# Loading K, wq and wo one stretch ahead, and a new order for the last head pair, in a one-core attention kernel

## The chip, the cores and the metric

The kernel runs on one core of a Trainium2 chip. The metric is the device time of one launch, in microseconds (us). "Span" is the stretch of the profile from the first to the last instruction, about 2 us shorter than the device time.

Engines are named as the profile names them: PE is TensorE (matmul), PEld its weight loads, DVE is VectorE, ACT is ScalarE, POOL is GpSimd, SP is SyncE. SPq, the queue of SP, issues nearly all DMAs of this kernel; they go out in program order, one after the other.

## The reference, cut to what matters

```python
xn = layernorm(x)                                # x: 2048 x 640, bf16
q  = xn @ wq                                     # 32 heads of 192
k, v = last 512 rows of k_cache, v_cache         # per head, 512 x 192
p  = softmax(q @ k.T * 192 ** -0.5)
s  = concat_heads(p @ v) @ wo                    # 6144 -> 640
g  = silu((silu(xn @ w_gate) * (xn @ w_up)) @ w_down)   # F = 1536
out = x + s * g
```

## The kernel before: the parts that matter

First comes the feed-forward part (until 168 us; it leaves `g2` in SBUF), then 16 pairs of heads. In a pair, PE computes scores for 4 contexts of 512 query rows (q for the next context is made between them), then PV for the 4 contexts, with output tiles (`wo_tile`) of two contexts earlier in between. K is centred over its rows, which needs K transposed (DMA transposes into `KT`), a sum of each of 3 chunks on DVE (`sum_k`) and an addition (`centre_k`).

```python
    for pr in range(NPAIR):                      # 16 pairs
        for b in range(NB):                      # 4 contexts
            i = pr * NB + b
            if b == 0:
                if pr < last:
                    load_k(pr + 1)
                load_v(pr)
                if pr < last:
                    load_wq(pr + 1)
                load_wo(pr)
                if pr >= last - 1:
                    for t in range(8):
                        load_xr(t + 8 if pr < last else t)
                        # ... (cut)
            for kc in range(KC):
                if kc < 3 and i + 1 < NS:
                    q_rows(i + 1, kc)            # PE, then a reduce on DVE into qT
                scores(i, kc)                    # PE, then an exp on ACT
                if pr < last:
                    if b == 1:
                        transpose_k(pr + 1, kc)  # a DMA transpose on SPq
                    elif b == 2 and kc < 3:
                        sum_k(pr + 1, kc)        # DVE
                    elif b == 3:
                        centre_k(pr + 1, kc)     # DVE
                        # ... (cut)
        # ... PV and output tiles of this pair (cut)
    i = last * NB
    for b in range(NB):                          # the last pair
        for q2 in range(2):
            if b >= 2:
                while stores:
                    store()                      # SPq
                wo_last(b - 2, 2 * q2)
                wo_last(b - 2, 2 * q2 + 1)
            pv(i + b, q2)                        # PE; O_b on ACT; transpose of O_b on SPq
```

An output tile of the last pair, `wo_last`, multiplies on DVE (`s_f`), adds on POOL or DVE, and writes into one of three `ob` buffers, which come free when their store has landed.

The softmax here doesn't subtract the row's maximum and nothing guards it: scores larger than these inputs give would overflow.

## Time and profile before

| | before |
|---|---|
| device time, median of 4 (range) | 963.70 us (963.48 to 966.59) |
| span | 962.5 us |
| PE busy / idle | 933.6 / 28.9 us |
| PE waits for the qT reduce | 12.6 us, 11 times |
| the one long wait in the tail | 5.5 us |

PE is the bottleneck. Part 1 of the page of the kernel before (busy time, share, instructions):

```profile
PE 933.6 (97%) x7970; PEld 588.0 (61%) x7970; DVE 572.0 (59%) x964; ACT 494.6 (51%) x867; POOL 63.6 (7%) x56
```

The Trainium skill (Perfetto Trace Analysis, section Identifying the Most-Contended Engine) warns that the busy share of matmuls says little about the distance to the limit. That holds here, so I measured how far apart matmuls *start* in undisturbed stretches: 108 ns on average for q and scores (they run in concurrent pairs of 64 rows, one pair every 216 ns), 83 ns for PV, 136 ns for output tiles. Whatever exceeds this is loss, including matmuls that count as busy but run at half clock.

The waits of PE in the kernel before (waiting engine and line, released by, total us, times, longest):

```profile
PE mm L415 <- DVE qT L420: 12.6, 11, 5.0
PE sc L491 <- DVE s_f L530: 5.5, 1, 5.5
PE mm L450 <- ACT O_b L460: 1.8, 3, 0.7
PE sc L429 <- ACT p_t L433: 0.7, 2, 0.5
```

The first line names the reduce, which takes 1.22 us and is not at fault. The timeline of the kernel before shows why it is late. In pair 14, which starts at 840.06 us, first the SP queue (start, duration in us):

```profile
842.04 1.46 SPq L93 DMA_DIRECT2D K_p<-in_A_k_cache_dram  x2
843.55 2.71 SPq L110 DMA_DIRECT2D V_p<-in_A_v_cache_dram  x2
846.30 3.28 SPq L104 DMA_DIRECT2D wq_p<-in_A_wq_dram  x5
849.63 0.52 SPq L117 DMA_DIRECT2D wo_p<-in_A_wo_dram  x1
850.20 4.19 SPq L482 DMA_DIRECT2D x_r<-in_A_x_dram  x8
854.57 5.10 SPq L130 DMA_TRANSPOSE KT<-K_p  x4
```

then DVE and PE in the same timeline (in brackets the idle time before, and what ended it):

```profile
860.85 0.69 DVE L137 TENSOR_REDUCE ssum<-KT 128x1 f32<-128x512 bf16 x1 [6.62 <-DMA KT<-K_p]
861.45 1.22 DVE L420 TENSOR_REDUCE qT<-mm 128x512 bf16<-128x1024 f32 x1
862.72 0.61 PE L415 MATMUL mm<-xnT,wq_p 64*128 64x512 bf16 x2 [5.01 <-DVE qT L420]
```

Read it backwards: PE waits 5.01 us for a reduce, the reduce stands behind a K sum on DVE, the K sum waits 6.62 us for a K transpose, and the transposes stand in the SP queue behind everything that the pair loads. In the ordinary pairs the x_r line is missing and PE waits at most 0.9 us (2.0 in pair 10).

The long wait of the tail, in the timeline of the kernel before:

```profile
919.67 13.64 SPq L464 DMA_TRANSPOSE OT_b<-O_b  x10
931.15 1.50 PE L450 MATMUL mm<-V_p,p_t 128*128 128x193 bf16 x16
933.40 1.00 SPq L537 DMA_DIRECT2D out_dram<-ob  x2
935.50 0.83 DVE L532 TENSOR_TENSOR ob<-s_f,sacc 128x640 bf16<-128x640 f32 x1 [5.76 <-DMA out_dram<-ob]
938.16 3.36 PE L491 MATMUL sc<-wo_p,OT_b 128*128 128x320 bf16 x12 [5.52 <-DVE s_f L530]
```

The DVE add waits for an `ob` buffer, so for a store, and the first store is issued at 933.40 only, behind ten transposes of O_b in the SP queue. Meanwhile the DVE can serve nothing else, and PE runs out of score buffers.

Both waits have a sequel. After them matmuls run at half clock: the 12 matmuls at 938.16 take 3.36 us, 1.79 elsewhere. The windows view of the kernel before (busy us of PE, PEld, DVE, ACT, POOL, then the granted clock, DMA share, GB/s):

```profile
857.00:868.00 11.00, 5.99 (x34) 2.44 (x31) 5.78 (x8) 2.96 (x3) 0.00 (x0) 0.72 0.16 31
931.00:942.00 11.00, 5.48 (x36) 3.85 (x34) 3.62 (x8) 2.92 (x8) 1.61 (x2) 0.77 0.38 106
```

The Trainium skill (TensorE: Matmul & The Clock Gate, Part 1) describes a gate that halves the array's clock after idleness and releases it after some 3.4 us of work. On the halving this trace agrees: after the wait in pair 14, pairs of matmuls start 427 ns apart, and 216 ns apart later. The release came after 5.9 us of work there, and after 3.3 us in pair 10.

### The profile page before, as it was taken

The page shows a single profiled execution, that of the slowest core. Times are in us where ns is not written, and L with a number is a line of the kernel's source. Part 1 is how long each engine was busy: PE and PEld are TensorE (multiplying, and loading weights), DVE is VectorE, ACT ScalarE, POOL GpSimd, SP SyncE. Part 2 cuts the span into 40 slices and gives each one's busy share as a digit, 9 for nine tenths or more (in the row PEclk, how much of TensorE's full clock was granted, in tenths as well). Part 3 has the DMA queues.
Part 4 walks back from the last instruction along what each step waited for, and adds up shares of the span by engine and source line. Part 5 has one row for each costly group of instructions (what it writes and reads, how often), then busy time and mean ns, then how long its engine had stood idle before and what let it go on. Part 6 is the DMA issues. An engine that isn't in the chain of part 4 may idle for free.

```text
span 962.5 us, 18723 instructions
## 1 busy us (share of the span) xinstructions
PE 933.6 (97%) x7970; PEld 588.0 (61%) x7970; DVE 572.0 (59%) x964; ACT 494.6 (51%) x867; POOL 63.6 (7%) x56
## 2 busy tenths in 40 slices
PE   9999999999999999999999999999999999979978
PEld 5455556575757575757575757574747474737555
DVE  6433320757666766666667666666676767656625
ACT  3222223666465646465646564645464646445651
POOL 0000000000000000000000000000000000006944
PEclk9999999999999999999999999999999999999998
DMA  9230500044434354535343434343343536362423
GB/s 299 57 72 20 119 17 1 1 73 85 85 74 80 78 85 73 86 72 91 68 88 70 92 66 86 71 86 72 62 97 58 100 56 102 54 158 33 126 56 104
DMA packets 240227, 76.32 MB, mean 79 GB/s; under 512 B 221200, under 2 KB 240144, under 8 KB 240144
## 3 DMA queue, kind: packets, MB, share of 16 engines
q1 hardware_dynamic: 239200, 74.32, 38.9%
q8 instruction: 62, 1.02, 0.4%
q10 hardware_dynamic: 944, 0.82, 0.3%
q14 instruction: 21, 0.17, 0.1%
HBM read 39.45 MB, written 2.62 MB: 44 GB/s over the span
## 4 chain that ended last, share of the span: by engine, by line
PE 81%; SPq 7%; DMA 5%; DVE 4%; issue 1%; ACT 1%; POOL 0%; DVEq 0%; ACTq 0%; POOLq 0%
PE sc L491 21%; PE mm L450 17%; PE mm L415 15%; PE sc L429 11%; PE sc L270 11%; PE mm L292 5%; SPq L130 4%; DMA KT<-K_p 4%; DVE qT L420 3%; SPq L104 2%; ACT O_b L460 1%; SPq L464 0%; DMA x_r<-in_A_x_dram 0%; ACT p_t L433 0%; DMA out_dram<-ob 0%
## 5 line engine op out<-in xcount | busy, mean ns | idle before, releaser
L433 ACT ACTIVATE p_t<-sc 128x1024 bf16<-128x1024 f32 x256 | 254.9, 1022 | 155.0 <-PE sc L429 154.4
L420 DVE TENSOR_REDUCE qT<-mm 128x512 bf16<-128x1024 f32 x189 | 230.9, 1222 | 95.9 <-PE mm L415 95.2
L460 ACT ACTIVATE O_b<-mm,r 128x192 bf16<-128x192 f32 x512 | 186.7, 417 | 180.4 <-DVE r L458 115.8
L415 PE MATMUL mm<-xnT,wq_p 64*128 64x512 bf16 x1890 | 239.0, 380 | 13.3 <-DVE qT L420 12.6
L491 PE MATMUL sc<-wo_p,OT_b 128*128 128x320 bf16 x1488 | 224.5, 300 | 5.9 <-DVE s_f L530 5.5
L429 PE MATMUL sc<-qT,khat 64*128 64x512 bf16 x1536 | 201.7, 378 | 1.2 <-ACT p_t L433 0.7
L450 PE MATMUL mm<-V_p,p_t 128*128 128x193 bf16 x2048 | 192.8, 247 | 2.0 <-ACT O_b L460 1.8
L450 PEld LDWEIGHTS <-p_t 128*128 128x128 bf16 x2048 | 174.2, 97 | 17.8 <-issue 9.2
L491 PEld LDWEIGHTS <-OT_b 128*128 128x128 bf16 x1488 | 144.2, 98 | 54.5 <-issue 5.7
L415 PEld LDWEIGHTS <-wq_p 64*128 64x128 bf16 x1890 | 95.3, 95 | 125.0 <-issue 24.3
L506 DVE TENSOR_TENSOR sacc<-sacc,sc 128x640 f32<-128x640 f32 x216 | 165.5, 808 | 0.0
L429 PEld LDWEIGHTS <-khat 64*128 64x128 bf16 x1536 | 79.4, 95 | 94.2 <-issue 8.0
L458 DVE RECIPROCAL r<-mm 128x2 f32<-128x2 f32 x256 | 43.7, 171 | 151.8 <-ACT O_b L460 106.0
L278 DVE TENSOR_TENSOR hT<-sc,sg 128x512 bf16<-128x512 f32 x47 | 32.5, 692 | 86.5 <-ACT sg L277 86.5
L509 POOL TENSOR_TENSOR sacc<-sacc,g_73 128x640 f32<-128x640 f32 x16 | 22.1, 1404 | 782.9 <-ACT O_b L460 782.9
L277 ACT ACTIVATE sg<-sc 128x512 bf16<-128x512 f32 x47 | 28.1, 597 | 77.6 <-PE sc L270 77.6
L270 PE MATMUL sc<-xnT,wu_sb 128*128 128x512 bf16 (+1 forms) x245 | 58.7, 370 | 0.0
L270 PE MATMUL sc<-xnT,wg_sb 128*128 128x512 bf16 (+1 forms) x245 | 58.7, 370 | 0.0
L292 PE MATMUL mm<-wd_sb,hT 128*128 128x320 bf16 x384 | 56.6, 299 | 0.0
L137 DVE TENSOR_REDUCE ssum<-KT 128x1 f32<-128x512 bf16 x48 | 32.6, 679 | 34.7 <-DMA KT<-K_p 34.7
L292 PEld LDWEIGHTS <-hT 128*128 128x128 bf16 x384 | 37.6, 98 | 18.9
L270 PEld LDWEIGHTS <-wu_sb 128*128 128x128 bf16 x255 | 24.9, 98 | 26.9
(51 smaller groups left out, 215.2 us busy)
## 6 DMA issues: line engine op xcount, KB each, us to landing
wo_p<-in_A_wo_dram SPq DMA_DIRECT2D x16, 480.0 KB, 4.6
K_p<-in_A_k_cache_dram SPq DMA_DIRECT2D x32, 192.0 KB, 3.4
V_p<-in_A_v_cache_dram SPq DMA_DIRECT2D x32, 192.0 KB, 3.7
wq_p<-in_A_wq_dram SPq DMA_DIRECT2D x64, 80.0 KB, 3.5
wq_p<-in_A_wq_dram SPq DMA_DIRECT2D x16, 160.0 KB, 3.7
x_r<-in_A_x_dram SPq DMA_DIRECT2D x16, 160.0 KB, 4.0
out_dram<-ob SPq DMA_DIRECT2D x16, 160.0 KB, 1.8
x_t<-in_A_x_dram SPq DMA_DIRECT2D x14, 160.0 KB, 3.0
```

What stands on the lines that cost most here:

```text
L130: nc.sync.dma_start_transpose(out=d["KT"][:, 0:3, j * P : (j + 1) * P], in_=d["K"][:, j, :, :].rearrange("p h d -> p (h d)"),)
L270: nc.tensor.matmul(out, w_sb[:, c, f * P : (f + 1) * P], xnT[:, c, qc], start=(c == 0), stop=(c == NC - 1),)
L292: nc.tensor.matmul(dn[:, 0:HD], hTs[b][:, f, ti * P : (ti + 1) * P], wd_sb[:, f, cols], start=(f == 0), stop=(f == NF - 1),)
L415: nc.tensor.matmul(q_ps[:, h, :], pairs[pr]["wq"][r, c, j * P : (j + 1) * P], xnT[r, c, b * 512 : (b + 1) * 512], start=(c == 0), stop=(c ...
L420: nc.vector.reduce_sum(qTs[i][:, j, :], q_ps[:, :, :].rearrange("p h n -> p n h"), axis=AX.X)
L429: nc.tensor.matmul(sc[:, h, :], khat[r, j, ks], qT[r, j, :], start=(j == 0), stop=(j == 2))
L433: nc.scalar.activation(p_t[:, :, :], sc[:, :, :], ACT.Exp, scale=scale)
L450: nc.tensor.matmul(acc[:, k, h * 256 : h * 256 + Dh + 1], Ps[i][kc][:, h, qt * P : (qt + 1) * P], V_p[:, kc, h, 0 : Dh + 1], start=(kc == ...
L458: nc.vector.reciprocal(r[:, k, :, :], a_k[:, :, Dh : Dh + 1])
L460: nc.scalar.activation(O_b[:, qt, h, :], a_k[:, h, 0:Dh], ACT.Copy, scale=r[:, k, h, :])
L491: nc.tensor.matmul(sc[:, n, 0:HD], OTs[i][:, 3 * qt + j, :], pairs[i // NB]["wo"][:, j, n * HD : (n + 1) * HD], start=(first and j == 0), ...
L506: nc.vector.tensor_tensor(s_t, s_t, sc[:, :, 0:HD], ALU.add)
```

## The change

The intent: K, wq and wo of the next pair are loaded during the PV stage before (or the feed-forward part), so that at the start of a pair the SP queue holds the K transposes first. In the last pair three contexts of PV come ahead of the first output tile; the first eight output tiles are written into the x_r tiles, which are done with by then, and not into shared buffers; O_b of these contexts is transposed two row tiles at a time, so by 6 DMA transposes and not 12; POOL takes more adds; the last context's first scores use PSUM buffers that q no longer needs; DVE normalises half of O_b; the last tile is handled in halves.

```diff
-                elif b == 3 and f < 5:
-                    centre_k(0, f)
+                elif b == 3:                     # feed-forward part
+                    if f < 5:
+                        centre_k(0, f)
+                    elif f < 8:
+                        (load_k, load_wq, load_wo)[f - 5]((1, 1, 0)[f - 5])
 ...
-        sc = sc_tile()
+        sc = mm_tile() if i == NS - 1 and kc < 2 else sc_tile()
 ...
+            if k == 0 and (i < 2 or (pr == last and b < NB - 1)):
+                nc.vector.tensor_tensor(O_b[...], a_k[...], r[...].to_broadcast([P, 2, Dh]), ALU.mult)
+                continue
 ...
-            if pr == last and b < NB - 1:        # a transpose for each row tile (3 blocks)
+        if pr == last and b < NB - 1:            # one for each two row tiles (6 blocks)
 ...
-            if b == 0:
-                if pr < last:
-                    load_k(pr + 1)
-                load_v(pr)
-                if pr < last:
-                    load_wq(pr + 1)
-                load_wo(pr)
-                # ... x_r loads
 ...
-                    if b == 1:
+                    if b == 0:
                         transpose_k(pr + 1, kc)
 ...
+            if b == 0:                           # after the context's scores
+                load_v(pr)
+                # ... x_r loads
 ...                                              # in the PV stage, after context b
+            if b == 0 and pr + 2 < NPAIR:
+                load_k(pr + 2)
+            elif b == 1 and pr + 2 < NPAIR:
+                load_wq(pr + 2)
+            elif b == 2:
+                load_wo(pr + 1)
 ...
-        ob = finp.tile([P, D], bf, name="ob", bufs=3)
+        ob = xrs[t] if b < 2 else finp.tile([P, D], bf, name="ob", bufs=4)
 ...
+    for b in range(NB - 1):
+        for q2 in range(2):
+            pv(i + b, q2)
+    for q2 in range(2):
+        wo_last(0, 2 * q2, G)
+        wo_last(0, 2 * q2 + 1, G)
+        pv(i + 3, q2)
+    for qt in range(4):
+        wo_last(1, qt, G)
+        store(3)
+        wo_last(2, qt, V if qt % 2 else G)
+        transpose_o(i + 3, qt)
+    for qt in range(4):
+        store(2)
+        wo_last(3, qt, G if qt < 2 else V)
+    store(0)
```

More of the change, by code (lines that the diff above doesn't have):

```diff
@@ L458, in pv @@
             nc.vector.reciprocal(r[:, k, :, :], a_k[:, :, Dh : Dh + 1])
+            if k == 0 and (i < 2 or (pr == last and b < NB - 1)):
+                nc.vector.tensor_tensor(
+                    O_b[:, qt, :, :], a_k[:, :, 0:Dh], r[:, k, :, :].to_broadcast([P, 2, Dh]),
+                    ALU.mult,
+                )
+                continue
             for h in range(2):
@@ L462, in pv @@
                 )
-            if pr == last and b < NB - 1:
-                nc.sync.dma_start_transpose(
-                    out=OT_b[:, 3 * qt : 3 * qt + 3, :],
-                    in_=O_b[:, qt, :, :].rearrange("p h d -> p (h d)"),
-                )
-        if pr < last and q2 == 1:
+        if pr == last and b < NB - 1:
+            nc.sync.dma_start_transpose(
+                out=OT_b[:, 6 * q2 : 6 * q2 + 6, :],
+                in_=O_b[:, 2 * q2 : 2 * q2 + 2, :, :].rearrange("p t h d -> p (t h d)"),
+            )
+        elif pr < last and q2 == 1:
             nc.sync.dma_start_transpose(
@@ L486, in late, with wo_mm @@
         return i // NB >= NPAIR - 2 and i % NB >= 2
-    def wo_mm(sc, i, qt, first=True, end=True):
-        for n in range(2):
-            for j in range(3):
-                nc.tensor.matmul(
-                    sc[:, n, 0:HD], OTs[i][:, 3 * qt + j, :],
-                    pairs[i // NB]["wo"][:, j, n * HD : (n + 1) * HD],
-                    start=(first and j == 0), stop=(end and j == 2),
-                )
+    def wo_mm(ps, i, qt, n, first=True, end=True):
+        for j in range(3):
+            nc.tensor.matmul(
+                ps, OTs[i][:, 3 * qt + j, :], pairs[i // NB]["wo"][:, j, n * HD : (n + 1) * HD],
+                start=(first and j == 0), stop=(end and j == 2),
+            )
     def wo_tile(i, qt):
@@ L500, in wo_tile @@
         sc = sc_tile()
-        wo_mm(sc, i, qt)
+        for n in range(2):
+            wo_mm(sc[:, n, 0:HD], i, qt, n)
         s_t = sacc[:, t, :].rearrange("p (n d) -> p n d", n=2)
@@ L516, with wo_last, store @@
     stores = []
-    def wo_last(b, qt):
+    def wo_last(b, qt, eng):
         i, t = last * NB + b, 4 * b + qt
-        end = b == NB - 1 and qt == 3
-        ob = finp.tile([P, D], bf, name="ob", bufs=3)
-        s_f = finp.tile([P, 2, HD], f32, name="s_f")
-        ob2 = ob[:].rearrange("p (n d) -> p n d", n=2)
-        s_t = sacc[:, t, :].rearrange("p (n d) -> p n d", n=2)
-        g_t = g2[:, t, :].rearrange("p (n d) -> p n d", n=2)
-        sc = sc_tile()
-        if late(i):
-            wo_mm(sc, i - NB, qt, end=False)
-        wo_mm(sc, i, qt, first=not late(i))
-        nc.vector.tensor_tensor(s_f[:], sc[:, :, 0:HD], g_t, ALU.mult)
-        pool = qt < 3 if b < 2 else qt % 2 == 0
-        (nc.gpsimd if pool else nc.vector).tensor_tensor(ob2, s_f[:], s_t, ALU.add)
+        ob = xrs[t] if b < 2 else finp.tile([P, D], bf, name="ob", bufs=4)
+        s_f = finp.tile([P, 2, HD], f32, name="s_f", bufs=3)
+        halves = [slice(n * HD, (n + 1) * HD) for n in range(2)]
+        split = b == NB - 1 and qt == 3
+        sc = None if split else sc_tile()
+        ps = [(mm_tile()[:, 0, :] if split else sc[:, n, :])[:, 0:HD] for n in range(2)]
+        for n, cols in enumerate(halves):
+            if late(i):
+                wo_mm(ps[n], i - NB, qt, n, end=False)
+            wo_mm(ps[n], i, qt, n, first=not late(i))
+            if split:
+                nc.vector.tensor_tensor(s_f[:, n, :], ps[n], g2[:, t, cols], ALU.mult)
+        if split:
+            for n, cols in enumerate(halves):
+                nc.vector.tensor_tensor(ob[:, cols], s_f[:, n, :], sacc[:, t, cols], ALU.add)
+        else:
+            nc.vector.tensor_tensor(
+                s_f[:], sc[:, :, 0:HD], g2[:, t, :].rearrange("p (n d) -> p n d", n=2), ALU.mult
+            )
+            eng.tensor_tensor(
+                ob[:], s_f[:].rearrange("p n d -> p (n d)"), sacc[:, t, :], ALU.add
+            )
         stores.append((t, ob))
-    def store():
-        t, ob = stores.pop(0)
-        nc.sync.dma_start(out=out2[t * P : (t + 1) * P, :], in_=ob[:])
+    def store(left):
+        while len(stores) > left:
+            t, ob = stores.pop(0)
+            nc.sync.dma_start(out=out2[t * P : (t + 1) * P, :], in_=ob[:])
     for pr in range(NPAIR):
@@ L541 @@
             i = pr * NB + b
-            if b == 0:
-                if pr < last:
-                    load_k(pr + 1)
-                load_v(pr)
-                if pr < last:
-                    load_wq(pr + 1)
-                load_wo(pr)
-                if pr >= last - 1:
-                    for t in range(8):
-                        load_xr(t + 8 if pr < last else t)
-                        if pr == last:
-                            add_x(t)
             for kc in range(KC):
@@ L566 @@
                             centre_k(pr + 1, 4)
-        if pr < last:
-            for i in range(pr * NB, pr * NB + NB):
-                for q2 in range(2):
-                    pv(i, q2)
-                    if i >= 2:
-                        wo_tile(i - 2, 2 * q2)
-                        wo_tile(i - 2, 2 * q2 + 1)
+            if b == 0:
+                load_v(pr)
+                if pr >= last - 1:
+                    for t in range(8):
+                        load_xr(t + 8 if pr < last else t)
+                        if pr == last:
+                            add_x(t)
+        if pr == last:
+            break
+        for b in range(NB):
+            i = pr * NB + b
+            for q2 in range(2):
+                pv(i, q2)
+                if i >= 2:
+                    wo_tile(i - 2, 2 * q2)
+                    wo_tile(i - 2, 2 * q2 + 1)
+            if b == 0 and pr + 2 < NPAIR:
[4 more added lines that the diff above has]
+                load_wo(pr + 1)
     i = last * NB
-    for b in range(NB):
+    V, G = nc.vector, nc.gpsimd
+    for b in range(NB - 1):
         for q2 in range(2):
-            if b >= 2:
-                while stores:
-                    store()
-                wo_last(b - 2, 2 * q2)
-                wo_last(b - 2, 2 * q2 + 1)
-            pv(i + b, q2)
-    for b in (2, 3):
-        for qt in range(4):
-            wo_last(b, qt)
-            if b == 2:
-                transpose_o(i + 3, qt)
-            while len(stores) > (b < NB - 1):
-                store()
-    while stores:
-        store()
+            pv(i + b, q2)
+    for q2 in range(2):
[11 more added lines that the diff above has]
+    store(0)
 _INS = ['A_x', 'A_k_cache', 'A_v_cache', 'A_wq', 'A_wo', 'B_x', 'B_w_gate', 'B_w_up', 'B_w_down']
```

## The prediction

> **What bounds it now.** TensorE: the page gives PE 933.6 us busy of 962.5; DVE (59%), ACT (51%) and DMA (39%) have room. In undisturbed stretches of the timeline, q and score matmuls start 108 ns apart, PV 83, output 136. Measured against these, nearly all losses after 168 us lie in three places.
>
> 1. *Once a pair, in 13 of 15 transitions.* The waits name PE q <- DVE qT, 11 times, 12.6 us, longest 5.0. The reduce itself takes 1.22 us: in the timeline DVE stands at the K sum, behind a KT transpose that has not landed, and the reduce queues behind it. The four transposes stand in the SP queue behind K, V, wq, wo (and in pair 14 eight x_r loads), start 8.8 us into the pair, issue every 1.3 us and land after 2.4 to 4.3; the sum wants them about 12.6 us in. After the two long waits matmuls start 387 to 399 ns apart for 3 and 6 us. The Trainium skill (TensorE: Matmul & The Clock Gate, Part 1) says that idleness halves the clock; the trace agrees: granted clock 0.72 in 857 to 868 us. Together 21 to 22 us. Pairs 0 and 1 lose nothing there.
>
> 2. *The tail.* One 5.5 us PE wait at 932 us (named DVE s_f): the DVE add waits for an `ob` buffer, that for a store, and the store sits in SP behind transposes that wait for O_b. Then 3 us at half clock. The last scores wait for exps (0.85 us), the third PV for PSUM (0.7). Together 11.4 us.
>
> 3. *Pair 0's first PVs* wait 0.66, 0.41, 0.43 us.
>
> **What the change does.**
> - K, wq, wo come a stretch earlier, and KT transposes are issued in the first context: start about 2 us into the pair, last landing about 9, against 12.6 needed. No engine work is added. 21 us back, all critical.
> - The loads now share DMA with OT transposes (3.7 us to landing) in the PV stage. An output tile needs its transpose about 6 us after O_b. No new wait expected.
> - Last scores in free PSUM: 1.5 us earlier, partly returned, because exps end at the same time and hold up ACT. DVE takes half of O_b (estimate 0.54 us, from its 0.82 for 640 and 1.22 for 1024 elements). Freeing a PV buffer still takes about 2.1 us, with two buffers and 1.34 us per PV: waits of 0.8 to 1 us remain at every second PV there. Same in pair 0: only 0.4 us gained.
> - `ob` over x_r: the store wait and its half clock go. Twelve POOL adds of 1.54 us fit. I allow 0.7 us of score-buffer waits.
> - The end: the third-last add stays off the path, the second-last moves to DVE ahead of the split tile's four half operations: 0.3 us later than now, not earlier.
> Tail gain about 8.5 us.
>
> Sum 21.5 + 0.4 + 8.5 = 30 us. **Predicted 933 us, range 930 to 939; faster by over 2% 0.95, within 2% 0.045, slower 0.005.**
>
> **Signs.** Right: PE <- DVE qT gone from the waits; K sums not waiting for DMA; granted clock 1.0 around pair 14 and in the tail; no s_f wait over 1 us; PE 98 to 99% busy; PE <- ACT O_b of some 2 us in the last pair. Wrong: OT_b or wo waits on PE in PV stages; KT landing over 12 us into the pair.
>
> **What would make it wrong.** Loads delaying OT transposes; DVE, 5.7 us of work against 5.9 in the K-sum context, still holding PE; POOL or PSUM buffers binding the tail; a throttle once PE never rests.

## The result

| | before | after |
|---|---|---|
| device time, median of 4 (range) | 963.70 us (963.48 to 966.59) | 933.15 us (932.71 to 933.61) |
| span of the profile | 962.5 us | 931.0 us |
| pairs 1 to 14, first q matmul to that of pair 15 | 683.4 us | 661.4 us |
| start of the last q matmul to end of the last matmul | 46.58 us | 37.26 us |
| last matmul to end of span | 4.57 us | 4.63 us |

The ratio is 0.9676 (95% interval 0.9657 to 0.9695). Ratios here are the mean time of one kernel's fast runs over that of the other's of the same rounds, so not quite the ratio of the medians quoted. Stretches such as those in the table are read from start times of single matmuls in the trace; they repeat from run to run within some 0.02 us where nothing waits for a DMA, much better than whole times do.

The same part of the page, kernel after:

```profile
PE 921.9 (99%) x7970; PEld 580.1 (62%) x7970; DVE 576.8 (62%) x974; ACT 488.2 (52%) x847; POOL 66.6 (7%) x58
```

PE's busy time itself fell by 11.7 us with the same 7970 matmuls: mostly because none runs at half clock any more. The windows view of the kernel after, for the stretches that match the two shown above, grants the full clock (1.00 in the third column from the right):

```profile
843.00:854.00 11.00, 11.00 (x107) 6.84 (x104) 8.58 (x16) 7.34 (x10) 1.10 (x1) 1.00 0.01 1
904.00:926.00 22.00, 22.00 (x179) 16.34 (x178) 15.45 (x22) 5.42 (x14) 18.11 (x12) 1.00 0.37 116
```

Its waits, all of them, kernel after (the second and fourth lie outside the change):

```profile
PE mm L453 <- ACT O_b L469: 1.9, 4, 0.6
PE sc L209 <- DVE zero_t L173: 1.2, 1, 1.2
PE sc L499 <- DMA OT_b<-O_b: 0.8, 1, 0.8
PE mm L418 <- ACT g_73 L296: 0.5, 1, 0.5
```

Pair 14 again, in the timeline of the kernel after (it starts at 825.90 us):

```profile
827.83 6.04 SPq L130 DMA_TRANSPOSE KT<-K_p  x4
833.97 1.24 SPq L110 DMA_DIRECT2D V_p<-in_A_v_cache_dram  x2
835.26 3.93 SPq L491 DMA_DIRECT2D x_r<-in_A_x_dram  x8
839.99 0.68 DVE L137 TENSOR_REDUCE ssum<-KT 128x1 f32<-128x512 bf16 x1
840.58 1.22 DVE L423 TENSOR_REDUCE qT<-mm 128x512 bf16<-128x1024 f32 x1
```

The transposes are first, the sum follows its turn without a bracket, so without waiting. Every pair from 1 to 14 is now 47.24 us long, to a hundredth.

The tail in the timeline of the kernel after: scores in free PSUM ("mm"), six PV parts in a row, then output tiles:

```profile
890.63 1.46 PE L432 MATMUL mm<-qT,khat 64*128 64x512 bf16 x12
891.93 1.46 PE L432 MATMUL sc<-qT,khat 64*128 64x512 bf16 x12
893.32 2.84 PE L453 MATMUL mm<-V_p,p_t 128*128 128x193 bf16 x32
896.66 2.83 PE L453 MATMUL mm<-V_p,p_t 128*128 128x193 bf16 x32 [0.50 <-ACT O_b L469]
900.04 2.83 PE L453 MATMUL mm<-V_p,p_t 128*128 128x193 bf16 x32 [0.55 <-ACT O_b L469]
902.71 1.79 PE L499 MATMUL sc<-wo_p,OT_b 128*128 128x320 bf16 x12
```

### A relation read from the traces

For each pair I noted when the first K sum starts, counted from the pair's first q matmul, and how long the pair is. All pairs that lose nothing are 47.24 us long. Kernel before, six of the fourteen pairs (the other eight lie on the same line, within 0.02 us):

| pair | first K sum starts at | pair length | loss against 47.24 |
|---|---|---|---|
| 1 | 15.14 us | 47.24 | 0 |
| 3 | 15.85 | 47.70 | 0.46 |
| 4 | 16.01 | 47.85 | 0.61 |
| 2 | 16.70 | 48.55 | 1.31 |
| 10 | 17.79 | 51.11 | 3.87 |
| 14 | 20.79 | 55.33 | 8.09 |

Undisturbed, the sum starts at 14.09 us. It may start up to 1.3 us late for nothing; past 15.4 us each microsecond costs one. Pairs 10 and 14 lose 1.5 and 2.7 us more than that, which is the half clock that follows their waits of 2.0 and 5.0 us. The length of the wait does not settle that alone: in e11_xr_behind (below) pair 10 waits 2.14 us and loses 2.53, just what the line says for a sum at 17.92 us. The windows view grants 1.00 of the clock there (660 to 672 us), and 0.86 around pair 10 of the kernel before (658 to 670). In the kernel after the transposes land 8.4 to 10.3 us into the pair.

### The profile page after: what moved, and what is told of

Read it like the earlier page. It is cut to its first block, busy times and chain, and to the rows that moved or that the text cites. A ratio compares the mean times of both kernels' runs of the same rounds, so it can differ in the third digit from the quotient of the medians.

```text
span 931.0 us, 18708 instructions
## 1 busy us (share of the span) xinstructions
PE 921.9 (99%) x7970; PEld 580.1 (62%) x7970; DVE 576.8 (62%) x974; ACT 488.2 (52%) x847; POOL 66.6 (7%) x58
## 4 chain that ended last, share of the span: by engine, by line
PE 98%; ACT 1%; DMA 0%; DVE 0%; issue 0%; DVEq 0%; ACTq 0%
PE sc L499 22%; PE mm L418 22%; PE mm L453 18%; PE sc L432 17%; PE sc L270 11%; PE mm L292 6%; PE sc L209 1%; ACT p_t L436 1%; DMA OT_b<-O_b 0%; PE mm L305 0%; ACT O_b L469 0%; PE mm L270 0%; PE tp L251 0%; DVE O_b L463 0%; DVE s_f L539 0%
## 5 line engine op out<-in xcount | busy, mean ns | idle before, releaser
L469 ACT ACTIVATE O_b<-mm,r 128x192 bf16<-128x192 f32 x492 | 180.3, 417 | 172.5 <-DVE r L461 107.9
L418 PE MATMUL mm<-xnT,wq_p 64*128 64x512 bf16 x1890 | 235.2, 376 | 0.5 <-ACT g_73 L296 0.5
L432 PE MATMUL sc<-qT,khat 64*128 64x512 bf16 x1524 | 195.7, 376 | 0.0
L418 PEld LDWEIGHTS <-wq_p 64*128 64x128 bf16 x1890 | 91.7, 94 | 112.0 <-issue 4.7
L432 PEld LDWEIGHTS <-khat 64*128 64x128 bf16 x1536 | 75.5, 94 | 90.2
L517 POOL TENSOR_TENSOR sacc<-sacc,g_73 128x640 f32<-128x640 f32 x16 | 22.1, 1406 | 760.8 <-ACT O_b L469 760.8
L270 PEld LDWEIGHTS <-wg_sb 128*128 128x128 bf16 x255 | 24.9, 98 | 23.3 <-issue 0.2
```

The source lines that it names most:

```text
L270: nc.tensor.matmul(out, w_sb[:, c, f * P : (f + 1) * P], xnT[:, c, qc], start=(c == 0), stop=(c == NC - 1),)
L418: nc.tensor.matmul(q_ps[:, h, :], pairs[pr]["wq"][r, c, j * P : (j + 1) * P], xnT[r, c, b * 512 : (b + 1) * 512], start=(c == 0), stop=(c ...
L432: nc.tensor.matmul(sc[:, h, :], khat[r, j, ks], qT[r, j, :], start=(j == 0), stop=(j == 2))
L469: nc.scalar.activation(O_b[:, qt, h, :], a_k[:, h, 0:Dh], ACT.Copy, scale=r[:, k, h, :])
```

## The experiments

The theory: two separate causes. (1) K transposes late because of what stands ahead of them in the SP queue. (2) In the tail, an output buffer whose store stands behind transposes, plus smaller PSUM waits. Rivals: one shared cause; DVE's own load (5.7 us of work in a context of 5.9 us); the early load, not the order, as what pays; the order of PVs, not the buffer, as what ends the wait of the tail. Twelve kernels ran, on three chips. The kernel before scatters from chip to chip and run to run (958.0 to 969.4 us in all), because its losses hang on when DMAs land, so small differences are taken from stretches in the trace.

### The two halves apart: e1_k_alone and e2_tail_alone

```diff
# e1_k_alone: the kernel before, with the new loads and transpose_k in context 0; tail as before
# e2_tail_alone: the kernel after, with loads and transposes of the kernel before
```

> The kernel before with the loading part alone: K, wq, wo loaded a stretch ahead, K transposed in the pair's first context, the old tail. My theory (late K transposes cost 21 to 22 us, tail separate): about 942 us, the PE wait on DVE qT gone, the 5.5 us wait at the tail's third output tile still there. Rival (the two parts share one cause, such as the SP queue or the DMA engines, so one part takes most of the gain): under 938 us.

> The kernel before with the tail part alone (all PVs ahead, output in x_r, adds on GpSimd, last scores in free PSUM, half of O_b on DVE), K loaded and transposed as before. My theory: about 955 us, the once-a-pair PE waits on DVE qT unchanged at 12 to 13 us in the waits view. Rival (one shared cause): under 950 us. The two gains should add up to the whole 30.5 us within 1 us.

e1: 943.08 us (942.79 to 943.52), before 965.13, ratio 0.9776. Its pairs 1 to 14 take 661.39 us, exactly as in the kernel after, and its tail keeps its old length (46.98 us from last q to last matmul) and its old wait of 5.9 us on s_f. e2: 951.32 us (948.32 to 955.78), ratio 0.9864, lower than the 955 expected, and with a wide range. Its tail is that of the kernel after (37.27 us). Two of its four runs, 948.32 and 948.59, even lie in the range of the rival (under 950), and the waits on qT did not stay at 12 to 13 us. The waits of e2:

```profile
PE mm L415 <- DVE qT L420: 8.7, 10, 4.3
```

Its profiled run, the fastest at 948.32, loses 15.8 us in pairs 1 to 14 where the profile of before lost 22.0, at the same relation (a sum at 15.58 us costs 0.19, at 16.32 costs 0.92, at 20.04 costs 7.16, half clock included). So in this run the shortfall comes from K transposes that landed earlier; why they did is not shown. The halves are separate, and the gains do not share a cause, since e1 keeps the old tail and e2 the old relation between late sums and lost time. That they sum to 30.5 us within 1 us, as I wrote, the times do not bear out (22.1 and 13.8 us, 35.9 together, with a kernel before that scatters); the stretches give 22.0 from the pairs and 9.3 from the tail, 31.3 together.

### What in the first half pays: e3_kt_second and e4_reorder_only

```diff
# e3_kt_second, against the kernel after
-                    if b == 0:
+                    if b == 1:
                         transpose_k(pr + 1, kc)
# e4_reorder_only, against the kernel after: no load a stretch ahead
+            if b == 0 and pr < last:             # before the context's scores
+                load_k(pr + 1)
+                load_wq(pr + 1)
 ...                                              # transpose_k in b == 0, then:
                 load_v(pr)
+                load_wo(pr)
 ...                                              # loads in feed-forward and PV stage removed
```

> The changed kernel with its early loads, but the K transposes back in the second context, so behind the V load, and in pair 14 behind eight x_r loads too. My theory (a pair loses only what the K sum starts after 15.4 us into the pair, whatever stands in the queue): transposes land about 11 to 12 us in, no loss in pairs 1 to 13, a sum near 15.5 us and at most 0.5 us lost in pair 14: 933 to 934 us. Rival (transposing first is needed beside the early loads): 0.4 us or more lost in every pair, 939 us or more.

> The changed kernel with no load a stretch ahead: at the start of a pair the SP queue gets K, wq, then the four K transposes, then V, wo, x_r. My theory (order in the queue is the cause): K lands about 7 us in, the transposes land about 13 us in, before 15.4, so nothing is lost: 933 to 935 us. Rival (a transpose fed by a load of the same pair is too late, the early load is what pays): 0.5 to 1.5 us lost in every pair, 941 us or more.

e3: 934.04 us, e4: 933.98 us, against 933.15 of the kernel after, and in both every pair from 1 to 14 is 47.24 us long. They were run at other times. In e3 the transposes land 9.8 to 11.2 us in, 14.8 in pair 14. In e4, which loads nothing earlier than the kernel before did, they land 13.0 to 14.8 us in, and DVE does wait for some of them, for nothing lost. Pair 5 of e4 in the timeline (starting at 401.35):

```profile
403.23 1.60 SPq L93 DMA_DIRECT2D K_p<-in_A_k_cache_dram  x2
404.87 4.74 SPq L104 DMA_DIRECT2D wq_p<-in_A_wq_dram  x5
409.77 5.09 SPq L130 DMA_TRANSPOSE KT<-K_p  x4
415.29 1.24 SPq L110 DMA_DIRECT2D V_p<-in_A_v_cache_dram  x2
416.13 0.69 DVE L137 TENSOR_REDUCE ssum<-KT 128x1 f32<-128x512 bf16 x1 [0.61 <-DMA KT<-K_p]
```

So each of the two measures of the change is enough alone: to load a stretch ahead, or to put the transposes ahead of V, wo and x_r. What counts is whether they land before 15.4 us. Both together buy 5 us of slack instead of 0.6.

### DVE as the rival: e8_sums_twice

```diff
# against the kernel after
                     elif b == 2 and kc < 3:
                         sum_k(pr + 1, kc)
+                        sum_k(pr + 1, kc)
```

> The changed kernel with each K sum taken twice (same result), 2.0 us more of VectorE in the third context of a pair, K on time. The sum may start up to 1.3 us later than its undisturbed 14.09 us without loss; the extra work puts VectorE 0.68, 1.35 and 2.03 us behind, so 0.5 to 0.9 us should be lost in each of 15 pairs: 941 to 946 us. Rival (VectorE has room, only a late transpose can hold TensorE): under 935 us. If it were VectorE's load and not the late transposes that bound the kernel before, the loss would be the whole 2 us a pair, 960 us or more.

943.11 us (942.49 to 943.90). Every pair from 1 to 14 is 47.87 us long, a loss of 0.63 us, with the first sum on time at 14.09 us. The waits of e8:

```profile
PE mm L418 <- DVE qT L423: 4.9, 15, 0.3
```

So DVE in that context has room for about 1.4 us more work (estimate: the 2.03 added less the 0.63 lost), not for 2.03. Its load was not the cause in the kernel before (the kernel after does the same DVE work there and loses nothing), but it is the next limit.

### What in the tail pays: e5_k_and_ob, e6_last_scores_sc, e7_ob_on_act

```diff
# e5_k_and_ob: e1_k_alone, and
-        ob = finp.tile([P, D], bf, name="ob", bufs=3)
+        ob = xrs[t] if b < 2 else finp.tile([P, D], bf, name="ob", bufs=3)
# e6_last_scores_sc: the kernel after, and
-        sc = mm_tile() if i == NS - 1 and kc < 2 else sc_tile()
+        sc = sc_tile()
# e7_ob_on_act: the kernel after, and
-            if k == 0 and (i < 2 or (pr == last and b < NB - 1)):
+            if k == 0 and i < 2:
```

> The kernel before with the loading part, and of the tail part one thing alone: the first eight output tiles are written into the x_r tiles instead of three shared buffers; order of the PVs, stores and adds as before. My theory (the 5.5 us wait is a wait for an output buffer whose store stands in the SP queue behind transposes, and the 3 us of half clock follow from it): 8 to 9 us faster than the loading part alone, about 934.5 us, no PE wait on DVE s_f over 1 us. Rival (the order, all contexts ahead of the first output tile, is what counts): 940 us or more, the wait on s_f still over 2 us.

> The changed kernel, but the last context's scores in the two usual score buffers. My theory (the exps of ScalarE end at the same time anyway, so most of what the free PSUM wins is lost again at the next PV buffer): 0.3 to 0.7 us slower than the changed kernel. Rival (the free PSUM is worth the whole 1.5 us of the old wait): 1.2 us or more slower.

> The changed kernel, but in the last pair ScalarE normalises all of O_b again. ScalarE then needs about 1.6 us for a PV against 1.34 on TensorE, and starts late behind the exps: about 0.9 us slower than the changed kernel (0.5 to 1.3). Rival (with contexts leading there is room enough): under 0.2 us slower.

> The changed kernel unaltered, as the yardstick for the three others of this call, whose differences are expected to be under 3 us: 932.5 to 934.5 us.

| | time, median (range) | last q to last matmul |
|---|---|---|
| e1_k_alone (old tail) | 943.08 (942.79 to 943.52) | 46.98 us |
| e5_k_and_ob | 935.63 (935.16 to 935.70) | 39.51 |
| a1_changed_again (the kernel after) | 933.58 (932.69 to 937.01) | 37.26 |
| e6_last_scores_sc | 935.27 (934.66 to 936.47) | 38.81 |
| e7_ob_on_act | 935.01 (934.21 to 937.90) | 38.48 |

The buffer alone brings 7.5 of the 9.7 us by which the tail of e1 exceeds that of the kernel after; I had expected 8 to 9. The order of before stays in e5, and its wait on s_f shrinks to 0.6 us:

```profile
PE sc L494 <- DVE s_f L533: 0.6, 1, 0.6
```

So the buffer is the cause, as the theory had it, and the order of the PVs is not needed for this part. The other 2.25 us are left to the remaining changes of the tail together. e6 and e7 price two of them; the fewer, larger transposes and the order had no run of their own.

e6 contradicts me: I expected most of the 1.5 us of the free PSUM to be given back, 0.3 to 0.7 us net, and it is worth 1.55 us (38.81 less 37.26). The reason is in the timeline of e6. The two waits between PVs are there too, with the same length as in the kernel after:

```profile
891.47 1.74 PE L432 MATMUL sc<-qT,khat 64*128 64x512 bf16 x12 [0.47 <-ACT p_t L436]
893.41 1.74 PE L432 MATMUL sc<-qT,khat 64*128 64x512 bf16 x12 [0.20 <-ACT p_t L436]
895.08 2.84 PE L453 MATMUL mm<-V_p,p_t 128*128 128x193 bf16 x32
898.42 2.83 PE L453 MATMUL mm<-V_p,p_t 128*128 128x193 bf16 x32 [0.50 <-ACT O_b L469]
901.80 2.83 PE L453 MATMUL mm<-V_p,p_t 128*128 128x193 bf16 x32 [0.55 <-ACT O_b L469]
```

They are not the exps' doing. In the kernel after the last exp ends at 895.8 us and ACT's share of O_b is ready to start at about that time anyway: it starts 2.56 us after the first PV there, and 2.55 us after it in e6, where ACT had been idle for 1.43 us. The waits come from the time that a PV buffer needs to come free with only two of them, which does not depend on when the scores were done. So the whole 1.55 us is kept.

e7 costs 1.22 us in the stretch (0.9 expected): ACT alone on O_b makes the third PV wait 1.27 us where DVE's help leaves 0.50.

### One move in the kernel before: e11_xr_behind

```diff
# against the kernel before
-                if pr >= last - 1:               # x_r loads with the other loads
+                if pr == last:
 ...
+            if b == 1 and pr == last - 1:        # pair 14's behind its K transposes
+                for t in range(8):
+                    load_xr(t + 8)
```

> The kernel before with one thing moved: the eight x_r loads of pair 14 are issued behind that pair's K transposes instead of ahead of them. By the relation read from the traces (a pair loses what its K sum starts after 15.4 us, and the long wait brought half clock with it): the sum of pair 14 starts about 16.5 us in instead of 20 to 21, that pair loses about 1 us instead of 7 to 8: 6 to 7 us faster than before. Rival (x_r is only one of many loads, the next pair's loads hold the transposes as much): under 3 us.

957.10 us (954.59 to 959.39) against 960.86 for the kernel before in the same rounds, ratio 0.9957: 3.8 us, not 6 to 7. Pair 14 did what was expected: its sum starts at 16.21 us and it loses 0.81 us, against 8.09 in the profile of before. The interval of the ratio, 0.9936 to 0.9978, allows a gain of 2.1 to 6.1 us, so it decides neither for my 6 to 7 nor for the rival's under 3. The kernel before was faster on this chip (960.86 against 963 to 965 on the others), so it may have lost less in pair 14 there. Its granted clocks point that way, 0.992 to 0.995 in the eleven runs on this chip against 0.990 in the profiled one. No profile of it was taken on this chip, and this stays open.

### Carrying on: e9_further and e10_two_lead

The profile of the kernel after still shows a wait of 0.83 us for the first transpose of pair 0 and the waits of 0.50 and 0.55 us in the tail.

```diff
# both, against the kernel after: pair 0's first context is transposed in two halves
-        if pr == last and b < NB - 1:
+        if i == 0 or (pr == last and b < NB - 1):
# e9_further: last scores between the first four PVs (so no free PSUM for them), last adds alternate
-        sc = mm_tile() if i == NS - 1 and kc < 2 else sc_tile()
+        sc = sc_tile()
 ...
+                if i == NS - 1:
+                    pv(last * NB + kc // 2, kc % 2)
                 scores(i, kc)
 ...                                              # the PVs of contexts 0 and 1 go from the tail
-        wo_last(3, qt, G if qt < 2 else V)
+        wo_last(3, qt, V if qt % 2 else G)
# e10_two_lead: two contexts lead instead of three
+    for b in range(2):
+        for q2 in range(2):
+            pv(i + b, q2)
+    for b in range(2):
+        for q2 in range(2):
+            wo_last(b, 2 * q2, G)
+            wo_last(b, 2 * q2 + 1, G)
+            pv(i + 2 + b, q2)
 ...                                              # wo_last(1, qt, G) goes from the loop below
```

> The changed kernel carried on in three places where its profile still shows waits: the last context's scores stand between the first four PVs instead of ahead of them (waits of 0.5 and 0.55 us, and ScalarE's exps, gone: 1.0 to 1.3 us), pair 0's first context is transposed in two halves (its wait of 0.83 us gone: 0.7 to 0.8 us), the adds of the last four tiles alternate between VectorE and GpSimd (0.3 to 0.6 us). Together 2.0 to 2.7 us faster than the changed kernel, 930.5 to 931.5. Rival: GpSimd's 1.54 us add of the last tile but one now ends last, or the K load collides with the halved transposes, and under 1.2 us is won.

> The changed kernel with pair 0's first context transposed in two halves (as in e9_further, where it took 0.99 us off the way to the first output tile), and with two contexts leading in the last pair instead of three, so that output tiles stand where the third PV buffer wait was (0.55 us), while the scores stay ahead of the PVs, without the changes between half-height and full matmuls that cost e9_further some 0.2 us each time. The first output tile's transpose landed 2.8 us after issue in the changed kernel, 0.1 us too late for this order, so 0.2 us of a new wait. Expected: 1.0 + 0.35 us faster than the changed kernel, tail from the last q matmul to the last matmul 36.9 us against 37.26; 931.8 to 932.6 us. Rival (the PV buffer wait only moves to the next PV): tail 37.2 us or more.

| | time, median (range) | first PV to first output tile, pair 0 | last q to last matmul | last matmul to end |
|---|---|---|---|---|
| kernel after | 933.15 and 933.58 | 8.84 us | 37.26 us | 4.63 us |
| e9_further | 932.01 (931.46 to 933.06), with 933.58 | 7.85 | 36.73 | 4.63 |
| e10_two_lead | 931.01 (929.99 to 931.49), another chip | 7.85 | 36.10 | 4.33 |

The halved transpose gives 0.99 us in both. In e9 the PV waits of the tail are gone but only 0.53 us is won, for a reason that the timeline of e9 shows: one score group and one PV part take 2.20 us together, where back to back they would take 0.65 and 1.34.

```profile
891.27 0.82 PE L432 MATMUL sc<-qT,khat 64*128 64x512 bf16 x6
892.03 1.51 PE L453 MATMUL mm<-V_p,p_t 128*128 128x193 bf16 x16
893.47 0.82 PE L432 MATMUL sc<-qT,khat 64*128 64x512 bf16 x6
```

From the last score matmul to the first PV matmul is 308 ns instead of 212, and 95 ns are added on the way back. The Trainium skill (TensorEngine Tiling (Array Packing), Key Properties) says that a change of tiling mode drains the array. The 0.1 us each way fits that; that the drain is what takes it was not tried apart. e9 makes eight more such changes than the kernel after.

The end of e9 won nothing either, as the rival said. With no POOL add beside it DVE's add takes 0.83 us (935.50 in the kernel before, shown above). Its timelines beside a POOL add, first in the kernel after (920.54), then in e9 (922.55):

```profile
920.54 1.64 DVE L547 TENSOR_TENSOR ob<-s_f,sacc 128x640 bf16<-128x640 f32 x1
```

```profile
922.55 1.24 DVE L547 TENSOR_TENSOR ob<-s_f,sacc 128x640 bf16<-128x640 f32 x1
925.40 1.54 DVE L542 TENSOR_TENSOR ob<-s_f,sacc 128x320 bf16<-128x320 f32 x2
```

The Trainium skill (GPSIMD Engine Reference, the table row on SBUF interfaces) says that GpSimd shares them with VectorE and contends with instructions that have two SBUF inputs. This agrees: the add has two, and takes up to twice as long when a POOL add is under way, which itself keeps its 1.54 us. The multiplication, with one input in PSUM, stays at 0.82 us. The add looks held rather than slowed: in all traces, each of the 36 adds of 128x640 that started over 0.1 us before the end of a POOL add ended 0.68 us after that end, whether it had started 0.37 or 0.99 us before it (at 920.54 in the kernel after: POOL's ended at 921.50, DVE's at 922.18). In e9 POOL's last add, moved close to the end, slows the two half adds that end the kernel (1.54 us instead of 0.88).

e10 keeps scores and PVs apart, so it makes no extra changes. Its tail is 1.16 us shorter than that of the kernel after, more than the 0.35 expected: the transposes were in time (no wait of 0.2 us), and the short delays for score buffers near the end are gone too, because output tiles of the second context no longer stand between those of the third. Its end is 0.3 us shorter, since POOL is free earlier. By the three stretches it beats the kernel after by 2.45 us; the medians, from different chips, differ by 2.1 to 2.6 us. Both e9 and e10 gave correct results.

## Why the prediction was right

It gave 933 us, range 930 to 939; the kernel took 933.15. Point by point:

- **Pair transitions, 21.5 us expected, 22.0 found.** The mechanism, as read from the waits and the timeline of before, held. Two times in it were off without harm: the undisturbed sum starts at 14.1, not 12.6 us, and a further 1.3 us are free, so the slack is over 5 us and not 3 to 4. Transposes start 1.9 us into the pair and land at 8.4 to 10.3 (2 and 9 expected).
- **What in it pays.** The prediction took the change as one. e3 and e4 show that early loads and first place in the queue each give all of it.
- **Half clock.** Counted in, and gone: the mean granted clock is 1.000 (0.990 before), and 1.00 in both windows shown. The starts 387 to 399 ns apart, of which the prediction speaks, leave out the 28 to 40 ns between the two matmuls of a pair; from pair to pair it is 427. That a wait of 2 us brings half clock is not certain: pair 10 of e11 went without. No throttle came from PE never resting.
- **Loads beside the OT transposes of the PV stage.** No new wait in pairs 1 to 14, as expected. In pair 0 the wait for OT_b grew from 0.43 to 0.83 us.
- **Pair 0, 0.4 us expected, 0.07 found** (first PV to first output tile 8.91 before, 8.84 after). The PV waits shrank from 0.66 and 0.41 to 0.42 and 0.42, but the transposed O_b landed 4.2 us after issue instead of 3.8. The obvious guess, the K load issued behind it, does not fit the other traces: e2 and e4, with no K load there, have 4.05 and 4.11 us, and e1, with one, 3.79. The cause stays open; transposing in halves avoided the wait.
- **Tail, 8.5 us expected, 9.3 found, less 0.06 at the end.** The store wait and its half clock account for 7.5 of it (e5). The step that failed is "partly returned, because exps end at the same time and hold up ACT": the exps do end at the same time, but ACT's first share of O_b is not wanted before then, and the whole 1.55 us is kept (e6). The remaining PV waits were 0.50 and 0.55 us, not 0.8 to 1, and delays for score buffers some 0.6 us (by start times of output matmuls), near the 0.7 allowed. The end, expected 0.3 us later, came 0.06 later.
- **DVE's margin**, named as a danger, is real but not used up: e8 finds the edge between 1.3 and 2.0 us of added work per pair.

The size came out right because each loss was measured against the start-to-start time of undisturbed matmuls, and because pairs 0 and 1 of the kernel before already showed what a pair without the wait looks like. That it fell within 0.2 us is partly luck: the terms were off by 0.5, 0.3 and 0.8 us, which cancelled in part, and the kernel before scatters by some 10 us from run to run.

## What to carry to other kernels

When a wait names a short instruction, follow its engine's queue backwards: here PE waited for a reduce, which stood behind a sum, which stood behind a transpose, which stood behind unrelated loads in one in-order queue. Ask of each load by when its consumer can be late for free, and order the queue by that; an earlier load and a better order may each suffice, and what is past the deadline costs microsecond for microsecond, with half clock on top after some waits of 2 us or more. On the last stretch of a kernel, let no output buffer depend on a store that is queued behind something the same engines still have to produce.

## What the Trainium skill lacked or had wrong

- TensorE: Matmul & The Clock Gate, Part 1 (HAM oscillation): it warns of idle gaps over some 3.4 us. In the kernel before a wait of 2.0 us (pair 10) was enough: pairs of matmuls then started 427 ns apart instead of 216 for about 3 us, and the pair lost 1.5 us more than the late sum accounts for. In e11 a wait of 2.14 us at the same place was not followed by it, so such a wait is a risk and no rule.
- TensorEngine Tiling (Array Packing), Key Properties: that a change of tiling mode drains the array is stated without a size. Between score matmuls of 64 rows and PV matmuls of 128 rows e9 shows about 0.1 us in each direction, whatever part of it is the drain.
- GPSIMD Engine Reference: the row on SBUF interfaces gives the contention with two-input VectorE instructions no size (another page of the skill tells of a hold, without a time for such adds). Here a 128x640 f32 add on VectorE went from 0.83 us to as much as 1.67 us (e7) beside a GpSimd add, which kept its 1.54 us, and ended 0.68 us after it.
- DMA: Bandwidth & Descriptors: no time for the issue of short SBUF-to-SBUF transposes (for that kind, a table on trn3 has one of 8,192 tiles alone). Here one of 128x384 held the SP queue 1.25 us in the median and one of 128x1536 1.43 us, with 2.3 to 6.5 us from issue to landing; that queue time, some 5 us, is what four K transposes cost each pair.
